# Block-sparse attention with a token and channel mixer: the first pair's copies on other engines, its gate in two banks, and a list made anew by a changed planner

## The chip, the cores and the metric

The kernel runs on one core of one Trainium2 chip. The metric is the device time of one execution in microseconds (us); lower is better. The kernel before took 246.04 us (median of three executions, 245.96 to 246.89).

The core has five instruction streams that run side by side and meet through semaphores: TensorE (PE in the profile; its weight loads are PEld), VectorE (DVE), ScalarE (ACT), GpSimd (POOL) and SyncE (SP), which here only starts transfers. Each stream is executed in the order in which it is written. GpSimd starts transfers too: those that turn 32-bit floats into 16-bit ones on the way.

## The reference

For each of 4 batches and 8 heads, q, k and v are 768 rows of 64 numbers. The 768 keys form 12 blocks of 64. A query may look at its own block and at the three earlier (or own) blocks whose mean key has the largest product with it. The heads' outputs, side by side, then go through a mixer over tokens and one over channels.

```python
k_rep = k.reshape(B, H, n_blocks, block, D).mean(axis=3)
gate_scores = np.einsum('bhsd,bhnd->bhsn', q, k_rep)
gate_scores = np.where(causal, gate_scores, -1000000000.0)
top_idx = np.argsort(gate_scores, axis=-1)[..., -top_k:]
...
scores = scale * np.matmul(q, k.transpose(0, 1, 3, 2))
mask = mask & (pos[:, None] >= pos[None, :])
scores = np.where(mask, scores, -1000000000.0)
...
return np.matmul(attn, v).astype(np.float32)
...
xt = x.transpose(0, 2, 1)
h = np.maximum(xt @ w_tok1, 0.0) @ w_tok2
u = x + h.transpose(0, 2, 1)
h2 = np.maximum(u @ w_ch1, 0.0) @ w_ch2
return (u + h2).astype(np.float32)
```

## The kernel before

Two heads of one batch form a pair, so there are 16 pairs; pairs 0 to 3 are batch 0. `pair(p)` describes the work of one pair, and `mlp(b)` the channel mixer of one batch, which needs the four pairs of that batch.

**A pair, step by step.** q and k come in as 32-bit tiles `q32` and `k32` (lines 508 and 516, by SP; for pair 0 half of them by ACT). v comes in through GpSimd's transfer as 16-bit `VA` (line 525). For the early pairs TensorE turns k and q over, in two halves of 384 columns each (`transposed`, line 446), into a PSUM tile `pm`. From there VectorE sums k's blocks of 64 (line 553, `ks`), and "spread" (line 534) writes the 12 sums of each head into a zeroed tile, so that one matmul serves both heads. `QT` (line 603) is q copied out of PSUM in 32 bits; `KA` and `QA` hold the 16-bit operands of the scores. `q16` (line 620) casts QT into QA. For pair 0 k goes from PSUM straight into KA (line 569); for later early pairs it goes through `k16` and is copied on to KA (line 573).

The gate is TensorE's product of QT and the block sums (line 639, into `g`), a bias add (line 643), VectorE's sorted eight largest (line 670), a comparison with the third largest (line 683, `bn`) and a memset that clears the own block (line 690). The result is turned over by TensorE (line 710) and copied into twelve further rows of QA (line 715), and KA's matching rows hold -30000 at their block, so the mask is part of the score matmul (line 731). ScalarE takes the exponential (line 744), GpSimd clears the upper triangle (line 752), TensorE multiplies with VA (line 761), and the token mixer follows (lines 779, 793, 807).

**Pair 0 is cut** (`CUT = 1`): each of these steps up to the gate runs in two halves of the sequence, so that the first can begin when half of k and q is there. Both halves of its gate lie in one PSUM bank `g`.

**The order is planned.** Nothing is issued as it is described. `P.op` records a step with the engines that may do it, a cost on each (time on the engine, time until its result is there, and for a transfer the time on the DMA engines), what it reads and writes, and a due time `pr`. `Plan.run` then simulates the engines and lists the steps: at each turn the engine that can start earliest takes its ready step with the smallest due time. The engines' instruction streams follow that list. Due times are a pair's own time `t0`, which advances by `EARLY` us for each of the first four pairs and by `PACE` after them, less a lead from the table `L` (`kd`, `qd`, `vd` for the loads of k, q, v; with an `e` in front for pairs 0 to 3). A step with `port=True` on VectorE shares one resource with GpSimd's steps in the simulation. In it all transfers, SP's and GpSimd's, follow each other in one line (`dma_free`). Where TensorE's list would leave a gap before the first channel mixer, `fill` puts matmuls of zeros (line 899), whose result nobody reads.

PSUM has two tiles of two banks for scores (`sc`) and four of one bank (`pm`) for everything else; a step that touches a `pm` or `sc` tile on one engine waits for the other engines' earlier steps on the same tile (`P.alone`).

Of the kernel before, what the change touches and what calls it, by code (L numbers as in the profile page):

```python
# [29 lines left out]
def _layout(groups):  # L30
    col, diag, width, base = {}, [], [], [0]
    for g, banks in enumerate(groups):
        mine, w = [], 0
        for bk, pieces in enumerate(banks):
# [17 lines left out]
EARLY, PACE = 5.78, 16.48  # L52
L = dict(kd=28.39, qd=24.29, vd=11.04, kt=13.4, kr=28.62, ke=-12.17, qt=24.03, qe=-10.99, q16=7.68, g=11.64, b=22.27,
         k16=20.14, r=24.99, w1=-9.34, w2=-3.8, wc1=11.98, wc2=30.18, tok=11.05, ml=12.98, o0=-2.69, o1=2.1, o2=2.23,
         o3=-0.75, o4=-2.45, o5=-0.39, o6=-3.33, o7=-8.31, o8=-1.83, o9=0.42, o10=-4.09, o11=-5.38, o12=6.03,
         o13=-1.8, o14=0.66, o15=3.06, m0=-0.25, m1=4.0, m2=6.99, m3=2.31, th=5.48, bd=5.16, cu=0.88, cs=5.86,
         ua=3.23, ub=23.41, ku=26.38, k0=5.54, k1=3.72, qu=23.81, dq=5.5, qp=5.5, dk=6.49, va=-11.68, ekd=26.02,
         eqd=24.07, evd=9.12, ekt=15.03, ekr=34.55, eke=-11.24, eqt=24.03, eqe=-6.62, eq16=4.03, eg=11.13, eb=22.27,
         etok=17.72)
# [28 lines left out]
class Plan:  # L88
# [6 lines left out]
    DMA = 1.1  # L95
    HELD = {"DVE": 115.0, "ACT": 130.0, "POOL": 85.0}
# [32 lines left out]
    def run(self, on_slot_end=None, fill=None):  # L129
        free = dict(FREE)  # L130
        dma_free, lanes = 0.0, [0.0] * self.LANES
# [30 lines left out]
        def start(o, e):  # L162
# [3 lines left out]
            if e in ("SP", "ACT") and len(o.cost[e]) > 2:  # L166
                t = max(t, lanes[0])
# [23 lines left out]
        while ready:  # L191
# [47 lines left out]
            if len(o.cost[e]) > 2:  # L239
                begin = max(dma_free, t + occ)  # L240
                dma_free = begin + o.cost[e][2] * self.DMA
                o.end = dma_free + lat
                if e != "POOL":
                    lanes.pop(0)
                    lanes.append(o.end)
# [54 lines left out]
def kernel(  # L300
# [11 lines left out]
    nc = tc.nc  # L312
# [110 lines left out]
    def weight(name, dst, src, n, each, pr, after):  # L423
        b = Buf(None)
        W[name] = (b, 0)
        P.op({"POOL": (800.0, 2200.0, n * each / 16.0)}, lambda: nc.gpsimd.dma_start(out=dst, in_=src), rd=[after], wr=[(b, 0)], pr=pr)

    def weights(after):
        weight("w1", w1, moe_w_tok1.rearrange("(j p) t -> p j t", p=128), 768, 60, L["w1"], after)
        weight("w2", w2, moe_w_tok2.rearrange("(g p) s -> p g s", p=128), 256, 135, L["w2"], after)  # L430
        for c in range(NCC):
            weight(("wc1", c), wc1[:, c, :], moe_w_ch1[128 * c:128 * c + 128, :], 128, 247, L["wc1"] + c, after)
        for f in range(0, NFC, 3):
            weight(("wc2", f), wc2[:, f:f + 3, :], moe_w_ch2[128 * f:128 * f + 384, :].rearrange("(g p) c -> p g c", p=128),
                   384, 98, L["wc2"] + f / 3, after)
# [46 lines left out]
    def pair(p):  # L482
# [38 lines left out]
        if p < 3:  # L521
# [3 lines left out]
        P.op({"POOL": (1100.0, 2200.0, 1536 * 16.0 / 16)}, lambda: nc.gpsimd.dma_start(  # L525
            out=VA.t[:, :, :, 0:64], in_=vs.rearrange("x (j p) d -> p x j d", p=128)), wr=[(VA, 0)], pr=t0 - lead["vd"], not_before=5000.0)

# [4 lines left out]
        def spread(e, z):  # L532
            for x in range(2):
                ENG[e].tensor_copy(out=ks2b.t[64 * x:64 * x + 64, x, z], in_=ks3.t[64 * x:64 * x + 64, 0, z])  # L534

        if straight_k:
# [6 lines left out]
            for x in range(2):  # L543
                P.op({"POOL": (772.0, 820.0), "ACT": (721.0, 825.0), "DVE": (470.0, 555.0)}, lambda e, x=x: copy(ENG[e], KA.t[0:64, x, :], KT.t[64 * x:64 * x + 64]),
                     port=True, rd=[(KT, 0), (KT, 1)], wr=[(KA, (x, 0)), (KA, (x, 1))], io=f"S{2 * x}>S0", pr=t0 - lead["ke"])
            if not thirds:
                P.op({"POOL": (380.0, 450.0), "DVE": (160.0, 240.0)}, lambda e: spread(e, slice(0, NB)), rd=[(ks3, 0), (ks3, 1)], wr=[(ks2b, 0), (ks2b, 1)], pr=t0 - lead["kr"] + 0.1, io="S0>S0 S2>S2")
# [395 lines left out]
```

## Time and profile before

| | |
|---|---|
| median of three executions | 246.04 us |
| the profiled execution's own time | 246.32 us |
| its span, first to last instruction | 244.6 us |
| TensorE / VectorE / ScalarE / GpSimd busy | 238.1 / 170.4 / 160.6 / 128.2 us |
| bytes read from and written to HBM | 29.01 / 8.45 MB |
| granted TensorE clock | 1.00 throughout |

The span leaves out 246.32 - 244.6 = 1.72 us of the execution that lie before its first instruction or after its last. In the profile's rows the first number is a start in us where the view is in order of time, "x3" is a count, a bracket at the end of a row is idle time of that engine just before the row and what ended it, and "L639" is line 639 of the kernel before. Copies that pass through one helper are recorded at its lines 342 (ScalarE) and 344 (VectorE, GpSimd).

### The profile page before, as it was taken

To read this page: it belongs to the slowest core of one execution; us is meant where nothing else is said; L and a number is where in the kernel's file an instruction comes from. 1 tells how busy PE (TensorE), PEld (TensorE's weight loads), DVE (VectorE), ACT (ScalarE), POOL (GpSimd) and SP (SyncE) were. 2 spreads that over 40 slices of the span, in tenths; PEclk is the share of its full clock that TensorE was granted. 3 is DMA by queue.
4 is the path that set the end of the run, shared out by engine and by line. 5 is a ranking of instruction groups with operands and counts; after the bars stand their busy time and mean duration, and the time that the engine had idled before them with its cause. 6 is when DMAs were issued, how large, how long until landed. Compare 5 with 4: busy or idle time off the path is not lost.

```text
span 244.6 us, 6642 instructions
## 1 busy us (share of the span) xinstructions
PE 238.1 (97%) x2467; PEld 162.9 (67%) x2467; DVE 170.4 (70%) x546; ACT 160.6 (66%) x251; POOL 128.2 (52%) x263
## 2 busy tenths in 40 slices
PE   7799999999999999999999999999999999999995
PEld 7588878897656676567575666567755766554644
DVE  3889887877879999999999889968385632202112
ACT  3786978759587696788988675589724672360620
POOL 6188778878487583978796747676102110000000
DMA  8999999999899897879999899510213211112103
GB/s 158 201 203 215 207 171 182 173 132 177 133 83 168 158 148 142 186 150 178 161 138 168 186 166 126 151 53 3 64 46 111 79 32 46 43 43 86 46 18 110
DMA packets 124120, 30.82 MB, mean 126 GB/s; under 512 B 117652, under 2 KB 120596, under 8 KB 124088
## 3 DMA queue, kind: packets, MB, share of 16 engines
q1 hardware_dynamic: 94400, 22.89, 46.7%
q0 software_dynamic: 28064, 7.08, 32.8%
q10 hardware_dynamic: 1624, 0.43, 0.9%
q8 instruction: 19, 0.31, 0.6%
q14 instruction: 13, 0.11, 0.2%
HBM read 29.01 MB, written 8.45 MB: 153 GB/s over the span
## 4 chain that ended last, share of the span: by engine, by line
PE 91%; DMA 3%; DVE 3%; issue 0%; SPq 0%; POOL 0%; POOLq 0%
PE pm L827 26%; PE pm L849 25%; PE sc L731 14%; PE pm L761 9%; PE pm L779 4%; PE pm L793 4%; DMA k<-in_k_dram 3%; PE pm L639 2%; PE pm L654 2%; PE pm L446 2%; PE pm L710 1%; PE pm L899 1%; DVE ks L553 1%; DVE ks L534 1%; PE pm L807 1%; DVE m L670 1%
## 5 line engine op out<-in xcount | busy, mean ns | idle before, releaser
L744 ACT ACTIVATE E<-sc 128x1024 f16<-128x1024 f32 (+2 forms) x96 | 84.0, 917 | 22.7 <-PE sc L731 21.3
L827 PE MATMUL pm<-uT,wc 128*128 128x384 f16 x384 | 69.9, 326 | 0.0
L849 PE MATMUL pm<-wc,h 128*128 128x512 f16 (+2 forms) x312 | 68.8, 363 | 0.0
L752 POOL TENSOR_SCALAR_AFFINE_SELECT E<-E 128x256 f16<-128x256 f16 (+1 forms) x96 | 39.2, 416 | 43.2 <-ACT E L744 41.4
L835 ACT ACTIVATE h<-pm 128x384 f16<-128x384 f32 x71 | 34.5, 491 | 28.2 <-PE pm L827 28.0
L827 PEld LDWEIGHTS <-wc 128*128 128x128 f16 x384 | 36.0, 98 | 22.5
L731 PE MATMUL sc<-QA,KA 76*128 76x512 f16 (+3 forms) x264 | 48.2, 301 | 0.3 <-DVE QA L344 0.3
L849 PEld LDWEIGHTS <-h 128*128 128x128 f16 x312 | 28.4, 98 | 26.0
L853 DVE TENSOR_TENSOR os<-u,pm 128x512 f32<-128x512 f16 (+2 forms) x26 | 16.6, 640 | 33.9 <-PE pm L849 33.2
L731 PEld LDWEIGHTS <-KA 76*128 76x128 f16 x264 | 23.6, 98 | 14.5 <-issue 0.4
L761 PEld LDWEIGHTS <-E 128*128 128x128 f16 x672 | 24.9, 98 | 3.6
L761 PE MATMUL pm<-VA,E 128*128 128x65 f16 x672 | 26.1, 193 | 0.0
L796 DVE TENSOR_TENSOR u<-x,pm 128x384 f16<-128x384 f16 x32 | 16.5, 542 | 4.7 <-PE pm L793 4.7
L837 DVE TENSOR_SCALAR h<-pm 128x384 f16<-128x384 f32 x25 | 13.8, 554 | 8.5 <-PE pm L827 7.5
L768 DVE TENSOR_TENSOR x<-pm,rc 128x384 f16<-128x384 f32 x32 | 17.8, 555 | 0.9
L525 POOL DMA_DIRECT2D VA<-in_v_dram x16 | 16.8, 1051 | 0.4 <-issue 0.3
L793 PE MATMUL pm<-h,w 128*128 128x128 f16 x192 | 13.8, 219 | 0.0
L342 ACT COPY QA<-bnt 12x384 f16<-12x384 f16 x20 | 10.2, 508 | 5.3 <-DVE bnt L695 4.9
L670 DVE MAX8 m<-gm 128x8 f32<-128x12 f32 x160 | 13.2, 156 | 0.5
L779 PE MATMUL pm<-x,w 128*128 128x128 f16 x192 | 13.3, 219 | 0.0
L793 PEld LDWEIGHTS <-w 128*128 128x128 f16 x192 | 11.9, 98 | 1.9
L779 PEld LDWEIGHTS <-w 128*128 128x128 f16 x192 | 11.7, 98 | 2.0 <-DVE x L768 0.4
(79 smaller groups left out, 302.2 us busy)
## 6 DMA issues: line engine op xcount, KB each, us to landing
out_dram<-os SPq DMA_DIRECT2D x22, 256.0 KB, 2.5
q<-in_q_dram SPq DMA_DIRECT2D x42, 96.0 KB, 2.9
k<-in_k_dram SPq DMA_DIRECT2D x38, 96.0 KB, 3.8
VA<-in_v_dram POOLq DMA_DIRECT2D x16, 192.0 KB, 6.0
wc<-in_moe_w_ch_dram POOLq DMA_DIRECT2D x8, 384.0 KB, 6.6
k<-in_k_dram SPq DMA_DIRECT2D x12, 192.0 KB, 5.6
turn<-k SPq DMA_DIRECT2D x11, 192.0 KB, 2.1
uT<-turn SPq DMA_DIRECT2D x44, 48.0 KB, 2.0
```

What stands on the lines that cost most here:

```text
L525: P.op({"POOL": (1100.0, 2200.0, 1536 * 16.0 / 16)}, lambda: nc.gpsimd.dma_start(out=VA.t[:, :, :, 0:64], in_=vs.rearrange("x (j p) d -> p ...
L731: nc.tensor.matmul(out=s.t[:, at:at + 128 * m], lhsT=KA.t[:, x, 128 * kk:128 * kk + 128], rhs=QA.t[:, q0:q0 + m, x, :], start=True, stop=True)
L744: nc.scalar.activation(out=E.t[:, BASE[g_]:BASE[g_ + 1]], in_=s.t[:, 0:WIDTH[g_]], func=AF.Exp, scale=scale)
L752: nc.gpsimd.affine_select(out=o, in_=o, pattern=[[0, len(d)], [1, 128]], compare_op=ALU.is_ge, fill=0.0, base=0, channel_multiplier=-1)
L761: nc.tensor.matmul(out=t[:, jq, :], lhsT=E.t[:, cc:cc + 128], rhs=VA.t[:, x, kk, :], start=(kk == 0), stop=(kk == jq))
L768: P.op(dve(384), lambda a=a, rc=rc, x=x: nc.vector.tensor_tensor(out=xp.t[:, :, 64 * x:64 * x + 64], in0=a.t[:, 0:NJ * 65].rearrange("p (j ...
L779: nc.tensor.matmul(out=m1.t[:, 128 * t:128 * t + 128], lhsT=w1[:, j, 128 * t:128 * t + 128], rhs=xp.t[:, j, :], start=(j == 0), stop=(j == ...
L793: nc.tensor.matmul(out=m.t[:, 128 * j:128 * j + 128], lhsT=w2[:, t, 128 * (j0 + j):128 * (j0 + j) + 128], rhs=h1.t[:, t, :], start=(t == 0 ...
L827: nc.tensor.matmul(out=m.t[:, 0:HS], lhsT=wc1[:, c, 128 * f:128 * f + 128], rhs=uT.t[:, c].rearrange("p (a w) -> p a w", a=4)[:, :, 96 * i ...
L835: nc.scalar.activation(out=o, in_=w, func=AF.Relu)
L849: nc.tensor.matmul(out=m.t[:, 0:wide], lhsT=h2.t[:, f, 128 * jj:128 * jj + 128], rhs=wc2[:, f, w:w + wide], start=(f == 0), stop=(f == NFC ...
L853: P.op(dve(wide), lambda j=j, m=m, o=o, w=w, wide=wide: nc.vector.tensor_tensor(out=o.t[:, w:w + wide].rearrange("p (c d) -> p c d", d=128 ...
```

## The change

Six edits, and then the list that the planner makes of them:

1. Pair 0's four casts of QT into QA (`q16`) are GpSimd's alone; before, VectorE or ScalarE took them.
2. Pair 0's copies of k out of PSUM into KA (`kev`) and of q into QT (`qev`) are ScalarE's alone; before, VectorE or ScalarE.
3. The two halves of pair 0's gate have a PSUM bank each (`gs`).
4. "Spread" on VectorE is a `tensor_reduce` over groups of one element, in place of a copy.
5. The step that loads v stands after q's copies in the description, and for pair 0 it waits for QT's second half; before, it waited for nothing but 5 us of simulated time.
6. The simulation has a line of its own for GpSimd's transfers (`cast_free`): such a transfer starts `PREPARE` = 1.2 us after its issue, and pushes back the transfers of SP that are still under way by its own length. Costs of several steps are set anew, `port` goes from two kinds of copy and their VectorE price from 470 to 870, `EARLY` goes from 5.78 to 4, many leads change, and the second half of pair 0's block sums has its own (`kr1`).

```diff
-EARLY, PACE = 5.78, 16.48
-L = dict(kd=28.39, qd=24.29, vd=11.04, kt=13.4, kr=28.62, ke=-12.17, qt=24.03, qe=-10.99, q16=7.68, g=11.64, b=22.27,
-         k16=20.14, r=24.99, w1=-9.34, w2=-3.8, wc1=11.98, wc2=30.18, tok=11.05, ml=12.98, o0=-2.69, o1=2.1, o2=2.23,
...
+EARLY, PACE = 4, 16.48
+L = dict(kd=28.39, qd=26.24, vd=9.53, kt=8.11, kr=35.36, ke=-11.57, qt=26.16, qe=-10.47, q16=13.67, g=12.55, b=18.91,
+         k16=22.64, r=24.99, w1=-9.34, w2=-6.45, wc1=11.98, wc2=27.86, tok=4.11, ml=12.0, o0=-2.91, o1=2.1, o2=2.23,
...
+    PREPARE = 1200.0
...
             if len(o.cost[e]) > 2:
-                begin = max(dma_free, t + occ)
-                dma_free = begin + o.cost[e][2] * self.DMA
-                o.end = dma_free + lat
-                if e != "POOL":
+                span = o.cost[e][2] * self.DMA
+                if e == "POOL":
+                    begin = max(cast_free, t + occ + self.PREPARE)
+                    cast_free = begin + span
+                    o.end = cast_free + lat
+                    for x in sent:
+                        if x.end - lat > begin:
+                            x.end += span
...
+                    dma_free = max(dma_free, begin) + span
+                else:
+                    dma_free = max(dma_free, t + occ) + span
+                    o.end = dma_free + lat
...
-        P.op({"POOL": (1100.0, 2200.0, 1536 * 16.0 / 16)}, lambda: nc.gpsimd.dma_start(
-            out=VA.t[:, :, :, 0:64], in_=vs.rearrange("x (j p) d -> p x j d", p=128)), wr=[(VA, 0)], pr=t0 - lead["vd"], not_before=5000.0)
...
             for x in range(2):
-                ENG[e].tensor_copy(out=ks2b.t[64 * x:64 * x + 64, x, z], in_=ks3.t[64 * x:64 * x + 64, 0, z])
+                if e == "DVE":
+                    nc.vector.tensor_reduce(out=ks2b.t[64 * x:64 * x + 64, x, z], in_=ks3.t[64 * x:64 * x + 64, 0, z].rearrange("c (n w) -> c n w", w=1), axis=AX.X, op=ALU.add)
+                else:
+                    nc.gpsimd.tensor_copy(out=ks2b.t[64 * x:64 * x + 64, x, z], in_=ks3.t[64 * x:64 * x + 64, 0, z])
...
-                    def kev(e, t=t, i=i, x=x):
-                        copy(ENG[e], KA.t[0:64, x, halves(i)], t.t[64 * x:64 * x + 64, 0:HS])
-                    P.op({**dve(HS), **act(HS)}, kev, rd=[(t, 0), (ks3, i)] if cut else [(t, 0)], wr=[(KA, (x, i))], io=f"P{2 * x}>S0", pr=at(i, lead["ke"]))
+                    def kev(t=t, i=i, x=x):
+                        nc.scalar.copy(out=KA.t[0:64, x, halves(i)], in_=t.t[64 * x:64 * x + 64, 0:HS])
+                    P.op(act(HS), kev, rd=[(t, 0), (ks3, i)] if cut else [(t, 0)], wr=[(KA, (x, i))], io=f"P{2 * x}>S0", pr=at(i, lead["ke"]))
...
-            P.op({**act(HS), **dve(HS)}, qev, rd=[(t, 0)], wr=[(QT, i)], io="P0>S0", pr=at(i, lead["qe"]))
+            P.op(act(HS) if cut else {**act(HS), **dve(HS)}, qev, rd=[(t, 0)], wr=[(QT, i)], io="P0>S0", pr=at(i, lead["qe"]))
...
+        P.op({"POOL": (1100.0, 650.0, 1536 * 14.0 / 16)}, lambda: nc.gpsimd.dma_start(
+            out=VA.t[:, :, :, 0:64], in_=vs.rearrange("x (j p) d -> p x j d", p=128)), rd=[] if p else [(QT, 1)], wr=[(VA, 0)], pr=t0 - lead["vd"], not_before=5000.0)
...
-                P.op({"DVE": (300.0, 380.0), "ACT": (410.0, 510.0)} if cut else {"POOL": (772.0, 820.0)} if p < L["qp"] else
-                     {"POOL": (772.0, 820.0), "ACT": (721.0, 825.0), "DVE": (470.0, 555.0)},
-                     q16, port=True, rd=[(QT, i)] if cut else [(QT, 0), (QT, 1)], wr=[(QA, (x, 0, i))], io=f"S{2 * x}>S0", pr=at(i, lead["q16"]))
+                P.op({"POOL": (430.0, 480.0)} if cut else {"POOL": (772.0, 820.0)} if p < L["qp"] else
+                     {"POOL": (772.0, 820.0), "ACT": (721.0, 825.0), "DVE": (870.0, 955.0)},
+                     q16, rd=[(QT, i)] if cut else [(QT, 0), (QT, 1)], wr=[(QA, (x, 0, i))], io=f"S{2 * x}>S0", pr=at(i, lead["q16"]))
...
-        g = Buf(Rr)
+        gs = [Buf(Rr) for _ in parts]
+        g = gs[0]
...
-                def gate(z0=z0, z1=z1, nb=nb):
+                def gate(z0=z0, z1=z1, nb=nb, g=gs[i]):
...
```

63 lines of the change are left out of this document (34 added, 29 removed).

## The prediction

> **What bounds the kernel now.** I read the page first, then the span cut into stages, the matmuls of zeros by stage, and the chain of waits in the first 20 us.
>
> ```profile
> PE 238.1 (97%) x2467; PEld 162.9 (67%) x2467; DVE 170.4 (70%) x546; ACT 160.6 (66%) x251; POOL 128.2 (52%) x263
> ```
>
> Busy time, share of the span and instructions by engine. TensorE is the bound, but 97% also counts the matmuls of zeros. The stages (length; busy us and instructions of PE, PEld, DVE, ACT and POOL; granted clock; DMA share; GB/s) show where it isn't:
>
> ```profile
> 5.00:14.00 9.00, 6.56 (x63) 5.28 (x62) 8.01 (x32) 6.86 (x14) 2.00 (x5) 1.00 1.45 205
> 20.00:30.00 10.00, 10.00 (x121) 8.75 (x117) 8.66 (x34) 7.71 (x11) 7.58 (x13) 1.00 1.34 211
> 56.00:240.00 184.00, 183.99 (x1750) 116.21 (x1748) 125.42 (x374) 120.25 (x189) 88.99 (x174) 1.00 0.66 109
> ```
>
> and so do the zeros of line 899 alone (PE and PEld busy, clock, DMA share, GB/s):
>
> ```profile
> 5.00:10.00 5.00, 0.91 (x11) 0.75 (x11) 1.00 1.54 197
> 10.00:15.00 5.00, 0.59 (x5) 0.40 (x5) 1.00 1.33 216
> 15.00:20.00 5.00, 0.60 (x5) 0.29 (x5) 1.00 1.32 201
> 20.00:25.00 5.00, 1.27 (x18) 1.08 (x18) 1.00 1.20 209
> 25.00:30.00 5.00, 1.43 (x21) 1.24 (x21) 1.00 1.47 212
> 40.00:60.00 20.00, 0.90 (x11) 0.67 (x11) 1.00 1.15 166
> ```
>
> From 56 us to 240 us TensorE idles 0.01 us, with no zeros: whatever the new list does to the other engines there, it can win nothing visible, and each us that the beginning saves is a us off the end. The beginning holds two stretches of slack. From 5 to 14 us it is 9.00 - 6.56 = 2.44 us idle and 0.91 + 0.59 = 1.50 us of zeros: **3.94 us**. From 15 to 30 us it is 0.60 + 1.27 + 1.43 = **3.30 us** of zeros, and 0.90 us more comes before the first channel mixer. Together 8.14 us: more than that the change cannot take out after the first 5 us, unless the useful work itself shrinks, and its matmuls stay the same in number.
>
> The chain of waits (start, us, what) says what the first stretch waits for:
>
> ```profile
> 4.15 5.64 DMA k<-in_k_dram
> 9.93 0.53 PE pm L446 x3
> 10.48 0.56 DVE ks L553
> 11.18 0.46 DVE k L344
> 11.64 0.47 DVE ks L553
> 12.14 0.53 DVE ks L534
> 12.69 0.90 DVE ks L534
> 13.58 0.27 DVE QA L344
> 13.89 0.98 PE sc L731 x7
> ```
>
> First pair 1's k, in flight for 5.64 us; then VectorE, one step after the other; and inside it two copies of twelve columns that take 0.53 and 0.90 us. Only from 13.89 us is TensorE fed.
>
> **Part 1: spread by a reduction.** What such small copies take elsewhere, what GpSimd did meanwhile, and two reductions:
>
> ```profile
> L534 DVE COPY ks<-ks 64x6 f32<-64x6 f32 x4 | 0.7, 165 | 0.1
> 11.79 0.82 POOL L344 COPY KA<-k 64x768 f16<-64x768 f16 x1 [0.19 <-DVE k L344]
> 12.56 0.51 POOL L752 TENSOR_SCALAR_AFFINE_SELECT E<-E 128x384 f16<-128x384 f16 x1
> L553 DVE TENSOR_REDUCE ks<-pm 128x6 f32<-128x384 f32 x14 | 7.3, 549 | 4.1 <-PE pm L446 4.1
> L541 DVE TENSOR_REDUCE ks<-KT 128x12 f32<-128x768 f32 x9 | 8.5, 942 | 0.3
> 12.18 0.52 PE L446 MATMUL pm<-id,q 128*128 128x128 f32 x3 [0.59 <-DMA q<-in_q_dram]
> ```
>
> A small copy takes 165 ns where nothing holds it; the slow two lie over a GpSimd copy (from 11.79 to 12.61 us) and a triangle step after it, and the first ends about when the GpSimd copy does. I read this as an access that the two engines share. A reduction's price follows from the last two rows: 384 more columns cost 942 - 549 = 393 ns, 1.02 ns each, so the fixed part is about 157 ns and twelve columns take some 170 ns. If a reduction doesn't need the shared access, two cost 0.34 us in place of 1.43: **1.09 us**; if it does, 0. I take 1.0 us of VectorE's chain, but only 0.6 us of TensorE's time, because the transposes of pair 1's q (12.18 us, last row) come 2.2 us after those of its k (9.93 us) and its gate needs both.
>
> **Part 2: casts, copies and banks of pair 0.**
>
> ```profile
> 6.37 0.51 ACT L342 CAST QA<-QT 64x384 f16<-64x384 f32 x1
> 6.38 0.55 DVE L344 CAST QA<-QT 64x384 f16<-64x384 f32 x1
> L344 POOL CAST QA<-QT 64x768 f16<-64x768 f32 x15 | 12.3, 819 | 0.9 <-ACT QT L342 0.5
> L342 ACT COPY QT<-pm 128x384 f32<-128x384 f32 x7 | 3.3, 486 | 0.3 <-PE pm L446 0.3
> L344 DVE COPY QT<-pm 128x384 f32<-128x384 f32 x5 | 2.7, 552 | 0.1
> 8.53 0.37 PE L639 MATMUL pm<-ks,QT 128*128 128x24 f32 x2 [0.71 <-DVE bn L683]
> 11.48 0.12 POOL L690 MEMSET bn<- 64x6 f16 x1
> ```
>
> VectorE loses two casts of 0.55 us and one QT copy of 0.552 us out of the 8.01 us that it is busy between 5 and 14 us: 1.65 us. ScalarE loses two casts (0.51 us each) and takes the copy at 0.486 us, so it does not grow. GpSimd gets four casts of half of 768 columns, between 0.41 us (half of 819 ns) and 0.82 us each; I take 0.43, 1.7 us in all, in the idle time before its row at 11.48 us (it is busy 2.00 of 9 us). If that cover were gone, the last cast would hold up the second half's scores by at most 0.8 us. The two banks remove the 0.71 us for which the second gate stood behind VectorE's comparison; 0 if QT's second half is late anyway, since it is copied at the same time. Of the 1.65 + 0.71 us I take 0.9 us on TensorE's path: the halves of pair 0's k and q land one after the other and set a floor under the rest.
>
> The Trainium skill speaks against handing casts to GpSimd: its page GPSIMD Engine Reference (section Key points) calls VectorE structurally about twice as fast for elementwise work. By that rule a cast would be 2 x 0.55 = 1.1 us, four of them 4.4 us, an estimate that would delay the second half's scores by some 2 us. The trace does not agree for this operation: 819 ns for twice the columns of VectorE's 0.55 us.
>
> **Part 3: v later, k and q earlier.**
>
> ```profile
> q1 hardware_dynamic: 94400, 22.89, 46.7%
> q0 software_dynamic: 28064, 7.08, 32.8%
> VA<-in_v_dram POOLq DMA_DIRECT2D x4, 192.0 KB, 7.4
> 3.31 1.19 POOL L525 DMA_DIRECT2D VA<-in_v_dram  x1
> 7.79 0.47 ACT L342 COPY QT<-pm 128x384 f32<-128x384 f32 x1
> 17.25 0.23 PE L761 MATMUL pm<-VA,E 128*128 128x65 f16 x2
> ```
>
> The first two rows (packets, MB, share of 16 engines over 244.6 us) make GpSimd's transfers dear: 32.8% x 244.6 / 7.08 MB = 11.3 us per MB, so one v of 192 KB takes 2.2 us of all the DMA engines. Before, pair 0's v is issued at 3.31 us, ahead of pair 1's k. Now it waits for QT's second half, which ends at 8.26 us, or some 7.5 us with part 2. Pair 1's k and q lose a neighbour worth between 0 (they arrive by their own queue's depth) and 2.2 us; I take 1.2, of which 0.8 us counts, since parts 1 and 2 partly free the same wait. Startup in all: 0.6 + 0.9 + 0.8 = **2.3 us of the 3.94**.
>
> The price: in the first 30 us a v lands 7.4 us after its issue (third row, median of four). Issued at 8 to 9 us it is there at 15.4 to 16.4 us. Its first user is at 17.25 us, and moves to 15.0 us if all else is 2.3 us earlier. TensorE would stand there for 0.4 to 1.4 us: I take **0.6 us** lost, because the list can put other matmuls ahead. GpSimd's casts and the own-block memset are what is queued behind that issue of 1.19 us on its stream; the second half's memset is due no sooner than 9 us, so nothing waits.
>
> **Part 4: the new order.** Leads and EARLY bring the loads of v for pairs 1 to 3 ahead of pair 5's k. The due times by the two tables: v of pair 1 from 5.78 + 2.1 - 9.12 = -1.2 to -3.0, of pair 2 from 4.7 to 1.1, of pair 3 from 7.5 to 3.5; k of pair 5 from 10.8 to 3.7, q of pair 3 ahead of k of pair 4 where it was behind. In the trace pair 1's v goes out late:
>
> ```profile
> 25.55 1.02 POOL L525 DMA_DIRECT2D VA<-in_v_dram  x1
> 34.67 1.49 PE L761 MATMUL pm<-VA,E 128*128 128x65 f16 x42
> ```
>
> so pair 1's product with v, due after the scores, runs at 34.67 us, and between 20 and 30 us TensorE multiplies zeros for 2.70 us. Moved up, 42 matmuls of the product would fill 1.4 us of them and its token mixer more. Against it stands that DMA is saturated there (1.34, 211 GB/s): what goes ahead pushes something else back. Bounds: all 3.30 us gained, or, if the waits move here from the startup, 2.3 us lost. I take **0.6 us** gained. The zeros before the first channel mixer stay; the later casts whose port and price change are 0.8 us each (row of 819 ns) beside a TensorE that never idles, so 0, and that is also what one would cost if it came due late.
>
> **Sum.** -2.3 + 0.6 - 0.6 = -2.3 us. Against the profiled execution: span 244.6 - 2.3 = 242.3, plus 1.72 around it, 244.0; that execution lies 0.28 us above the median, so for the median 246.04 - 2.3 = **243.7 us**.
>
> **The rivals.**
> *GpSimd's transfers don't go ahead* (slower). The simulation lets a v transfer start 1.2 us after issue and run alone: 1.1 + 1.2 + 1.34 x 1.1 + 0.65 = 4.4 us until it is there, where the row above has 7.4. TensorE takes its list in order, so a product listed 4.4 us behind its load stands for up to 3.0. It decides once the list places a product less than 7.4 us after its v's issue with nothing in between. For pairs 0 and 1 that costs 3.0 us each and for pair 2, when the rush is ending, half as much: 7.5 us. Of these 2.7 take the place of zeros that stand there now, and 2.3 are what the start gains; 2.5 us remain: 248.5 us. Against it: the product at 17.25 us has no idle time before it now. The Trainium skill's page DMA: Bandwidth & Descriptors, section Issuing engines are not separate DMA queues, says that transfers from all engines share the same 16 DMA engines and interleave: by that, no transfer of GpSimd truly goes ahead, which is this rival's mechanism. The trace agrees: a DMA share of 1.34 between 20 and 30 us means packets of more than one transfer at a time on each engine.
> *DMA decides.* k, q and v of four pairs are the same bytes at 205 to 211 GB/s; TensorE is fed sooner but runs dry sooner, and the zeros of 15 to 30 us grow by most of what the start saves: 245.5 us. For it: a DMA share over 1 in each window quoted above up to 60 us. Against it: pairs 4 and 5 are loaded early now, and can move back.
> *Both stretches close.* The start gains 2.9 and the second stretch 2.0 us: 241.1 us.
> *The edits change nothing on the path*, since pair 1's landing alone sets 9.79 us: 246.0.
>
> **Chances.** Forecast 0.46 (242.6 to 244.8), DMA decides 0.20, both close 0.12, GpSimd's transfers 0.18, nothing 0.04. Half a percent, about what a measurement of this kernel can tell from no change, is 1.2 us, so faster is below 244.8: 0.45 of the forecast, 0.12, and 0.02 of the second rival, 0.59. Same gets the rest of it, the fourth and a little of the slower one: 0.24. Slower keeps 0.17. The range goes from the case where both close to a milder form of the slower one, with 1.6 us lost in place of 2.5: 241.0 to 247.6 us, with the forecast's own 242.6 to 244.8 inside.
>
> **What would show it.** Part 1: the spread rows of pair 1 at 0.2 us beside a busy GpSimd. Part 2: no idle time before the second gate; GpSimd casts of about 0.43 us. Part 3: pair 1's k landing before 9 us, the first score matmuls two us earlier, and little idle time before the first product with v. Part 4: fewer zeros from 15 to 30 us. I am wrong if TensorE idles before line 761 for over 2 us, if zeros from 15 to 56 us grow past 6 us, or if idle time appears after 56 us.

## The result, and the profile after

| | before | after |
|---|---|---|
| median (executions) | 246.80 us (6) | **253.12 us** (6) |
| lowest and highest | 245.96, 251.62 | 251.88, 254.25 |
| profiled execution, span | 246.32, 244.6 | 251.88, 250.2 |

The ratio is 1.0265 [1.0224, 1.0306]: slower, and above the predicted range of 241.0 to 247.6 us. Here and below the ratios leave out executions that lie over 1.5% above the fastest of their kernel (before, the one of 251.62 us), and the medians keep them. In the kernel after, the lines that the prediction names lie further down: scores L748, exponential L761, product with v L778, load of v L627, second token matmul L810, zeros L916, copies L355 (ScalarE) and L357 (VectorE, GpSimd).

The page of the kernel after, engines:

```profile
PE 237.4 (95%) x2432; PEld 160.9 (64%) x2432; DVE 174.0 (70%) x541; ACT 159.2 (64%) x249; POOL 128.2 (51%) x270
```

TensorE is busy 0.7 us less in a span that is 5.6 us longer. Matmuls of zeros fell from 9.12 to 6.73 us (both rows over the whole span):

```profile
0.00:250.00 250.00, 9.12 (x103) 7.60 (x103) 1.00 0.79 123
```
```profile
0.00:250.00 250.00, 6.73 (x68) 5.58 (x68) 1.00 0.79 123
```

So of the 5.6 us, idle time is +6.25 (12.75 in place of 6.5) and busy time -0.65. The zeros' 2.4 us can't be taken off the busy time one for one: the rows of single lines overlap, and add up to 286.6 us before, where TensorE is busy for 238.1. The stages of the kernel after (columns as in the prediction) show where it idles:

```profile
5.00:14.00 9.00, 8.31 (x83) 7.02 (x82) 6.30 (x30) 6.81 (x13) 5.27 (x12) 1.00 1.30 220
14.00:40.00 26.00, 20.90 (x278) 17.01 (x277) 20.08 (x80) 17.54 (x25) 19.04 (x31) 1.00 1.64 188
56.00:200.00 144.00, 141.02 (x1482) 92.05 (x1479) 123.08 (x367) 102.83 (x156) 87.97 (x180) 1.00 0.82 129
```

The first row is the gain that was forecast, in part: 0.69 us idle, where it was 2.44, so 1.75 of 2.3 us (the zeros there stay, 1.70 us where they were 1.50). The other two are the loss: 26.00 - 20.90 = **5.10 us** idle from 14 to 40 us and 144.00 - 141.02 = **2.98 us** from 56 to 200 us. The same two stretches before:

```profile
14.00:40.00 26.00, 25.84 (x339) 21.83 (x337) 21.81 (x93) 20.52 (x29) 21.57 (x39) 1.00 1.57 193
56.00:200.00 144.00, 143.99 (x1504) 94.11 (x1502) 118.18 (x362) 106.41 (x161) 88.99 (x174) 1.00 0.81 126
```

0.16 and 0.01 us. Zeros from 14 to 40 us fell from 3.30 to 1.67 us, so some of the idle time only takes their place: idle time and zeros together went from 3.46 to 6.77 us. What TensorE waits for after the change (in total, times, longest), and some of its rows before 40 us:

```profile
PE pm L778 <- DMA VA<-in_v_dram: 3.8, 3, 1.7
PE pm L778 <- DVE u L813: 2.0, 1, 2.0
PE pm L810 <- DMA w<-in_moe_w_tok_dram: 1.2, 1, 1.2
```
```profile
7.83 0.85 PE L656 MATMUL pm<-ks,QT 128*128 128x24 f32 x6 [0.20 <-ACT QT L355]
...
8.84 0.87 PE L459 MATMUL pm<-id,k 128*128 128x128 f32 x6
...
9.55 0.83 PE L748 MATMUL sc<-QA,KA 76*128 76x256 f16 x10
...
22.43 1.51 PE L778 MATMUL pm<-VA,E 128*128 128x65 f16 x42 [1.16 <-DMA VA<-in_v_dram]
...
30.42 0.51 PE L810 MATMUL pm<-h,w 128*128 128x128 f16 x6 [1.20 <-DMA w<-in_moe_w_tok_dram]
...
33.91 1.49 PE L778 MATMUL pm<-VA,E 128*128 128x65 f16 x42 [1.71 <-DMA VA<-in_v_dram]
...
36.77 0.83 PE L778 MATMUL pm<-VA,E 128*128 128x65 f16 x21 [0.94 <-DMA VA<-in_v_dram]
```

The start is 1.1 us earlier (pair 1's k is turned at 8.84 us, 9.93 before), but the first product with v goes from 17.25 to 22.43 us, and still waits. GpSimd's stream says why:

```profile
14.47 0.82 POOL L357 CAST QA<-QT 64x768 f16<-64x768 f32 x1
15.24 0.83 POOL L357 COPY KA<-k 64x768 f16<-64x768 f16 x1
16.01 1.19 POOL L627 DMA_DIRECT2D VA<-in_v_dram  x1
...
19.69 0.84 POOL L439 DMA_DIRECT2D w<-in_moe_w_tok_dram  x1
...
25.89 1.03 POOL L627 DMA_DIRECT2D VA<-in_v_dram  x1
```

Pair 0's v is issued at 16.01 us, behind pair 1's casts. Pair 1's v, which the change was to bring forward, goes out no earlier than before (25.55 us then), the first token weight later (14.81), and the second, for which TensorE waits, at 22.11 us (21.64). The 2.0 us in the second stretch are here, VectorE and GpSimd side by side:

```profile
128.01 0.42 POOL L769 TENSOR_SCALAR_AFFINE_SELECT E<-E 128x256 f16<-128x256 f16 x1
...
128.23 3.41 DVE L357 CAST QA<-QT 64x768 f16<-64x768 f32 x1
...
128.39 1.26 POOL L625 TENSOR_TENSOR R<-QT 128x640 f32<-128x640 f32 x1
...
129.98 1.24 POOL L664 TENSOR_TENSOR R<-R 128x640 bf16<-128x640 f32 x1
...
131.17 1.10 POOL L627 DMA_DIRECT2D VA<-in_v_dram  x1
131.57 1.00 DVE L813 TENSOR_TENSOR u<-x,pm 128x384 f16<-128x384 f16 x2
...
132.16 0.82 PE L778 MATMUL pm<-VA,E 128*128 128x65 f16 x21 [2.00 <-DVE u L813]
```

A cast that takes 0.56 us elsewhere lasts until GpSimd's chain of steps ends, and the sums behind it on VectorE (`u`) come so late that TensorE stands 2.00 us.

### The profile page after: what moved, and what is told of

Read it like the earlier page. It is cut to its first block, busy times and chain, and to the rows that moved or that the text cites. A ratio compares the mean times of both kernels' runs of the same rounds, so it can differ in the third digit from the quotient of the medians.

```text
span 250.2 us, 6570 instructions
## 1 busy us (share of the span) xinstructions
PE 237.4 (95%) x2432; PEld 160.9 (64%) x2432; DVE 174.0 (70%) x541; ACT 159.2 (64%) x249; POOL 128.2 (51%) x270
## 4 chain that ended last, share of the span: by engine, by line
PE 75%; DMA 10%; DVE 5%; issue 3%; ACT 2%; POOL 1%; SPq 1%; ACTq 0%; DVEq 0%
PE pm L844 24%; PE pm L866 22%; PE sc L748 11%; PE pm L778 7%; DMA VA<-in_v_dram 6%; PE pm L796 4%; PE pm L810 3%; DMA q<-in_q_dram 2%; ACT E L761 2%; DMA k<-in_k_dram 2%; PE pm L459 1%; PE pm L671 1%; DVE h L854 1%; DMA uT<-turn 1%; DVE m L687 1%
## 5 line engine op out<-in xcount | busy, mean ns | idle before, releaser
L761 ACT ACTIVATE E<-sc 128x1024 f16<-128x1024 f32 (+2 forms) x96 | 84.1, 917 | 24.3 <-PE sc L748 23.0
L852 ACT ACTIVATE h<-pm 128x384 f16<-128x384 f32 x74 | 36.1, 490 | 29.7 <-PE pm L844 29.3
L748 PE MATMUL sc<-QA,KA 76*128 76x512 f16 (+3 forms) x264 | 48.5, 301 | 0.4 <-ACT E L761 0.4
L748 PEld LDWEIGHTS <-KA 76*128 76x128 f16 x264 | 23.6, 98 | 14.2 <-issue 0.6
L778 PE MATMUL pm<-VA,E 128*128 128x65 f16 x672 | 26.1, 193 | 6.1 <-DMA VA<-in_v_dram 3.8
L778 PEld LDWEIGHTS <-E 128*128 128x128 f16 x672 | 24.9, 98 | 10.0 <-issue 5.8
L627 POOL DMA_DIRECT2D VA<-in_v_dram x16 | 16.9, 1054 | 0.1
L781 DVE RECIPROCAL rc<-pm 128x6 f32<-128x6 f32 x32 | 6.0, 187 | 14.3 <-PE pm L778 14.2
L357 POOL CAST QA<-QT 64x768 f16<-64x768 f32 (+1 forms) x17 | 13.3, 780 | 4.3 <-ACT QT L355 3.8
L854 DVE TENSOR_SCALAR h<-pm 128x384 f16<-128x384 f32 x22 | 12.1, 551 | 4.6 <-PE pm L844 2.3
L810 PE MATMUL pm<-h,w 128*128 128x128 f16 x192 | 13.8, 219 | 1.2 <-DMA w<-in_moe_w_tok_dram 1.2
L810 PEld LDWEIGHTS <-w 128*128 128x128 f16 x192 | 12.1, 98 | 3.4 <-DMA w<-in_moe_w_tok_dram 1.4
## 6 DMA issues: line engine op xcount, KB each, us to landing
out_dram<-os SPq DMA_DIRECT2D x22, 256.0 KB, 2.1
```

Source lines behind the costliest of these rows:

```text
L627: P.op({"POOL": (1100.0, 650.0, 1536 * 14.0 / 16)}, lambda: nc.gpsimd.dma_start(out=VA.t[:, :, :, 0:64], in_=vs.rearrange("x (j p) d -> p ...
L748: nc.tensor.matmul(out=s.t[:, at:at + 128 * m], lhsT=KA.t[:, x, 128 * kk:128 * kk + 128], rhs=QA.t[:, q0:q0 + m, x, :], start=True, stop=True)
L761: nc.scalar.activation(out=E.t[:, BASE[g_]:BASE[g_ + 1]], in_=s.t[:, 0:WIDTH[g_]], func=AF.Exp, scale=scale)
L778: nc.tensor.matmul(out=t[:, jq, :], lhsT=E.t[:, cc:cc + 128], rhs=VA.t[:, x, kk, :], start=(kk == 0), stop=(kk == jq))
L810: nc.tensor.matmul(out=m.t[:, 128 * j:128 * j + 128], lhsT=w2[:, t, 128 * (j0 + j):128 * (j0 + j) + 128], rhs=h1.t[:, t, :], start=(t == 0 ...
L852: nc.scalar.activation(out=o, in_=w, func=AF.Relu)
```

## The experiments

All ratios are against the kernel before, run on the same chip (medians 246.6 to 248.0 us). Differences between kernels are taken from ratios, 1% being 2.5 us. Idle time is TensorE's in the profiled execution, from windows as above.

| run | kernel | us | ratio |
|---|---|---|---|
| e4 | before + pair 0's engines, banks, reduction | 244.5 | 0.9895 [0.9842, 0.9948] |
| e5 | before + reduction alone | 245.9 | 0.994 [0.9917, 0.9963] |
| e11 | e4 + new prices and ports | 246.0 | 0.9966 [0.9936, 0.9995] |
| e10 | e4 + new line for GpSimd's transfers | 248.2 | 1.003 [0.9996, 1.0064] |
| e12 | e4 + new table | 255.1 | 1.0215 [1.0135, 1.0295] |
| e17 | e4 + table, first four pairs' half | 252.5 | 1.0145 [1.0072, 1.0217] |
| e18 | e4 + table, later pairs' half | 249.2 | 1.0092 [1.0061, 1.0122] |
| e7 | after, old line | 250.5 | 1.0148 [1.0079, 1.0218] |
| e8 | after, old table | 249.4 | 1.0089 [1.0052, 1.0127] |
| e1 | after, v of pair 0 first on GpSimd | 254.8 | 1.0285 [1.0211, 1.036] |
| e13 | after, v of pair 0 due before q of pair 2 | 256.0 | 1.0348 [1.0304, 1.0392] |
| e14 | e12, the same due time | 257.2 | 1.0197 [1.0108, 1.0287] |
| e16 | e13, and token weights due as early | 254.6 | 1.0219 [1.0147, 1.0291] |
| e15 | e13, transfers planned to land after 8.0 us | 253.7 | 1.0213 [1.0148, 1.0279] |
| e2 | after, GpSimd's first six transfers moved up | 249.5 | 1.0091 [1.0054, 1.0128] |
| e3 | after, five late casts by ScalarE | 250.6 | 1.0138 [1.0097, 1.0178] |
| e6 | e2 and e3 | 247.1 | 1.0023 [0.9984, 1.0063] |
| e9 | after, zeros ahead of four waiting steps | 253.2 | 1.023 [1.0185, 1.0275] |

### The edits without the new list

e5 takes the reduction alone; e4 adds the engines of pair 0's casts and copies and its two gate banks, with the old simulated line, prices and leads.

```diff
-ENG[e].tensor_copy(out=ks2b..., in_=ks3...)
+nc.vector.tensor_reduce(out=ks2b..., in_=ks3...)        # e5 and e4, on VectorE
-P.op({**dve(HS), **act(HS)}, kev, ...)
+P.op(act(HS), kev, ...)                                  # e4; qev alike
-{"DVE": (300.0, 380.0), "ACT": (410.0, 510.0)} if cut
+{"POOL": (430.0, 480.0)} if cut                          # e4
+gs = [Buf(Rr) for _ in parts]                            # e4
```

> The kernel before with one edit: VectorE's spread is a reduction in place of a copy (same list). If the copies wait for an access that GpSimd holds and a reduction doesn't need it: pair 1's two rows at 0.2 us in place of 0.53 and 0.90, and 245.4 to 246.0 us beside 246.0 to 246.5 of the kernel before. If a reduction waits as well or they are slow for themselves: rows of 0.5 us or more, no difference.

> The kernel before, with its planner, costs and due times, and of the change only the engines of pair 0's casts and copies, the gate's two banks and the spread by reduction. If these edits are good and the list alone costs the time: 244.0 to 245.8 us, TensorE fed by 12 to 13 us, no new waits for v. If the edits themselves cost it (GpSimd slower at casts, ScalarE overloaded, its transfers of v behind them): 247.5 us or more.

Both are faster than before, as expected. e4's stages:

```profile
5.00:14.00 9.00, 8.59 (x82) 7.49 (x81) 6.08 (x30) 7.26 (x15) 6.30 (x12) 1.00 1.49 207
14.00:40.00 26.00, 25.55 (x339) 21.44 (x339) 21.22 (x93) 21.03 (x30) 21.66 (x41) 1.00 1.64 196
56.00:200.00 144.00, 143.99 (x1512) 94.18 (x1511) 117.59 (x361) 105.95 (x160) 87.58 (x172) 1.00 0.78 124
```

The start is as full as after the change, and neither of the two later stretches idles. **e4 beats both kernels**: what makes the kernel after slow is in the planner's part.

### The planner's three parts, one at a time

e11 gives e4 the new prices and takes `port` from two kinds of copy; e10 gives it the new line for GpSimd's transfers; e12 the new table. In all three v's load also stands where the change puts it (edit 5).

```diff
-                     {"POOL": (772.0, 820.0), "ACT": (721.0, 825.0), "DVE": (470.0, 555.0)},
-                     q16, port=True, ...
+                     {"POOL": (772.0, 820.0), "ACT": (721.0, 825.0), "DVE": (870.0, 955.0)},
+                     q16, ...
```
```diff
-                begin = max(dma_free, t + occ)
-                dma_free = begin + o.cost[e][2] * self.DMA
+                    begin = max(cast_free, t + occ + self.PREPARE)
+                    cast_free = begin + span
...
-        P.op({"POOL": (1100.0, 2200.0, 1536 * 16.0 / 16)}, ...
+        P.op({"POOL": (1100.0, 650.0, 1536 * 14.0 / 16)}, ...
```
```diff
-EARLY, PACE = 5.78, 16.48
-L = dict(kd=28.39, qd=24.29, vd=11.04, kt=13.4, kr=28.62, ke=-12.17, qt=24.03, qe=-10.99, q16=7.68, g=11.64, b=22.27,
+EARLY, PACE = 4, 16.48
+L = dict(kd=28.39, qd=26.24, vd=9.53, kt=8.11, kr=35.36, ke=-11.57, qt=26.16, qe=-10.47, q16=13.67, g=12.55, b=18.91,
...
```

> The good kernel (244.5 us) and of the planner's changes only the prices: port gone from two kinds of copy, 870 for them on VectorE, and the small price changes. If the missing port is what holds up VectorE: casts of QT into QA on VectorE of 1.3 us or more beside GpSimd's steps, at least one of them ahead of a wait of TensorE, 245.5 to 248 us. If the cast of 3.41 us was bad luck of that one list: 244 to 245 us, no wait over 0.5 us after 56 us.

> The good kernel (before, with pair 0's edits and the spread, 244.5 us) and of the planner's changes only the simulated line for GpSimd's transfers; prices, port, due times as before. If the simulation alone makes the list too hopeful: TensorE waits 1 to 2 us for v between 20 and 40 us, 246 to 248 us. If it is harmless alone: 244 to 245 us.

> The good kernel (244.5 us) and of the planner's changes only the due times: L, EARLY, kr1. If they put pair 0's v behind GpSimd's copies for pair 1: v issued at about 16 us, its first product waits, and 246 to 249 us. If they are good and only the other two parts spoil the list: 243 to 245 us.

Over e4, the prices cost 0.7% (little more than the intervals allow), the line 1.35% and the table **3.2%**, more than either case expected. In e10 TensorE did not wait for v but 1.2 us for a token weight and 2.4 us, at 116 us, for a step of VectorE. e7 and e8 undo the line (second diff) and the table (third diff) from the other side, in the kernel after.

> The changed kernel with the old simulation of transfers (one line for all, GpSimd's results 2.2 us later, old lengths) and the new table, EARLY, costs and edits of pair 0. If the simulated transfers make the list too hopeful: no wait of TensorE for v or a token weight over 0.5 us, and 247 to 250 us (the late cast may remain). If the new due times are to blame: the waits for v stay, 252 us or more.

> The changed kernel with the due times and EARLY of the kernel before; the new simulation, costs and edits of pair 0 stay. If the simulated transfers make the list too hopeful: TensorE still waits over 2 us for v and token weights, 250 us or more. If the new due times are to blame: no such waits, 247 us or less.

The undone line saves 1.2% and the undone table 1.8%. Both came out between their two cases: one wait for v stayed in each, of 2.1 and 1.9 us. The parts don't add up: 5.25% one by one, 3.7% together. But the medians fall into two groups: 244.5 to 249.4 us with the old table, 250.5 to 257.2 us with the whole new one and nothing moved by hand. What of the prices is felt can be seen in VectorE's casts of QT (shortest, median, longest ns), in e11, where `port` is gone, and in e12, where it stays:

```profile
L345 DVE CAST QA<-QT x6: 531/736/2850, 57.2 to 161.3; 64x768 f16<-64x768 f32 x6
```
```profile
L345 DVE CAST QA<-QT x5: 542/556/816, 61.5 to 171.6; 64x768 f16<-64x768 f32 x5
```

With `port` kept (e4, e10, e12, e14, e17, e18) none took over 1.3 us; without it the longest took 0.87 us in e8, 2.85 in e11 and 3.41 in after. A held cast costs TensorE only where a step that it needs soon stands behind: in e11 all idle time from 56 to 200 us is 0.36 us.

e17 and e18 split the table: EARLY, the leads with an `e`, o0 to o3, cu, kr1, w2 and wc2 in e17; the others in e18.

```diff
-EARLY, PACE = 5.78, 16.48
+EARLY, PACE = 4, 16.48
-L = dict(... eqd=24.07, ekr=34.55, eke=-11.24, eqe=-6.62, eq16=4.03, eg=11.13, etok=17.72 ...)
+L = dict(... eqd=25.89, ekr=37.94, eke=-13.29, eqe=-7.22, eq16=2.64, eg=13.71, etok=19.71 ...)
```

> Pair 0's edits with the old simulated line and old prices, and of the new table only what concerns the first four pairs: EARLY = 4, their leads, their offsets, the lead of the second half's sums and the due times of the weights. If the loss arises where the first pairs' loads are placed, 250 to 255 us, with TensorE idle for over 2 us between 14 and 40 us and little idle time after 56 us. If it arises in the later pairs' leads, 244.5 to 247 us.

> The other half of the table: the later pairs' leads and offsets, with EARLY = 5.78 and the first four pairs as before. If the loss is the beginning's, 244.5 to 247 us; if it is made after 56 us, 248 us or more, with TensorE idle for over 2 us after 56 us.

e17, then e18:

```profile
14.00:40.00 26.00, 22.98 (x286) 19.32 (x285) 17.45 (x75) 18.18 (x28) 21.01 (x36) 0.93 1.52 193
56.00:150.00 94.00, 91.84 (x957) 60.31 (x954) 79.27 (x236) 72.67 (x110) 67.39 (x128) 0.98 1.03 152
```
```profile
14.00:40.00 26.00, 25.44 (x332) 21.16 (x331) 20.68 (x92) 20.26 (x30) 21.99 (x42) 1.00 1.54 196
56.00:150.00 94.00, 91.44 (x965) 59.96 (x964) 80.40 (x246) 72.38 (x109) 67.38 (x129) 1.00 1.12 164
```

The first pairs' half empties the beginning (3.02 us idle, and a granted clock of 0.93). The later pairs' half leaves it full (0.56 us), and yet TensorE idles 2.56 us after 56 us, where it never idled. Each half has a loss of its own: 2.5% over e4 in e17, 2.0% in e18. That e17 idles after 56 us too (2.16 us), against the expectation, would fit EARLY, from which the later pairs' due times count on; no run separates that.

Part of the loss comes with a lower clock. e17's six executions took 249.3 and 249.5 us at a mean clock of 1.0, and 252.2 to 254.1 us at 0.98 to 0.986; e12's four took 250.7 us at 1.0 and 254.3 to 256.1 us at 0.973 to 0.978. So some 5 to 6 us over e4 are lost at full clock too (in e12 by one execution), and 3 to 5 us more come where it falls.

### Which place in the order

e1 keeps the list of after and moves one load in it; the others change due times and have everything listed anew.

```diff
+    for name, by in [(("v", 0), 99000.0)]:
+        o = casts[name]
+        order.remove(o)
+        order.insert(next(i for i, x in enumerate(order) if x.eng == "POOL" and x not in casts.values() and x.start >= o.start - by), o)
```
e13, e15, e16 (in after) and e14 (in e12):
```diff
-pr=t0 - lead["vd"], not_before=5000.0)
+pr=t0 - lead["vd"] - (3.7 if p == 0 else 0.0), not_before=5000.0)
```
e16, and then e15, besides:
```diff
-768, 53, L["w1"], after)
+768, 53, -13.4, after)
-256, 119, L["w2"], after)
+256, 119, -13.2, after)
```
```diff
-        P.op({"POOL": (1100.0, 650.0, 1536 * 14.0 / 16)}, ...
+        P.op({"POOL": (1100.0, 4250.0, 1536 * 14.0 / 16)}, ...
```

> The changed kernel's list, step for step, but the issue of pair 0's v stands first on GpSimd's stream, as in the kernel before. Late transfers (the list issues GpSimd's transfers too late for the products that need them): the wait of 1.2 us at pair 0's product with v goes, and the time falls by about 1.3 us from 253 us. DMA decides (its engines are full, so an earlier v only makes k and q later): pair 1's k lands 1 to 2 us later, the first score matmuls come later than 9.6 us, and the time stays within 0.5 us of 253.

> The planner lets transfers start in the order of their due times. By the new table the loads of q of pair 2 (due -15.66), k of pair 4 (-13.87) and k and q of pair 3 (-13.44, -13.31) are due ahead of pair 0's v (-12.03); by the old one v (-11.81) stood ahead of all of them (-10.28, -7.72, -9.43, -7.48). Here v alone gets a due time between pair 2's k and q (-15.73), and everything is listed anew. If that place is the step that failed, v is issued at 8.3 to 8.6 us, the wait of 1.16 us before the first product goes, and the time is 250 to 251 us. If the new order as a whole is at fault (weights, v of pairs 1 to 3), v is issued as early, but the waits at 30 to 37 us stay and the time is 252 to 253 us.

> The kernel with the new table alone (old simulated line, old prices; 255.1 us) with the same due time for pair 0's v. If v's place is what makes the table dear, 249 to 251 us and v issued at 8.3 to 8.6 us. If other entries of the table are, 253 us or more with v issued as early.

> The kernel after with the due times of pair 0's v and of the two token weights set so that they stand among the loads of k and q where they stood before the change (-15.73, -13.4, -13.2). If the order of transfers is the cause, the wait of 1.2 us for a token weight goes too, and the time is 1 to 2 us below that of the kernel with v's due time alone, 248 to 249.5 us. If it isn't, the two agree within 0.7 us.

> The kernel after with that due time, and GpSimd's transfers planned to be there 8.0 us after their issue (the measured median of the first 40 us) in place of 4.4. If products listed too early behind their loads are a cause of their own, the waits for v at 30 to 37 us go (0.94 to 1.71 us each) and the time is 1.5 to 3 us below that of the kernel with the due time alone. If the list has nothing else to put ahead of them, zeros or other waits take their place, and the two times agree within 0.7 us.

My theory of v's place missed. In e1 the load goes out ahead of pair 1's k, and TensorE waits 0.84 us for that k:

```profile
10.18 1.51 PE L459 MATMUL pm<-id,k 128*128 128x128 f32 x6 [0.84 <-DMA k<-in_k_dram]
```

e14 is no better than e12 (1.0197 and 1.0215). In e13 v is out at 8.54 us and the first product runs at 15.65 us without a wait, yet the kernel is 0.8% *slower* than after:

```profile
15.65 0.83 PE L778 MATMUL pm<-VA,E 128*128 128x65 f16 x21
...
27.31 0.84 PE L796 MATMUL pm<-x,w 128*128 128x128 f16 x12 [1.67 <-DVE QA L357]
...
30.91 0.88 PE L810 MATMUL pm<-h,w 128*128 128x128 f16 x12 [0.80 <-DMA w<-in_moe_w_tok_dram]
...
34.73 2.47 PE L778 MATMUL pm<-VA,E 128*128 128x65 f16 x42 [2.75 <-DMA VA<-in_v_dram]
```

What the start gains is waited away later: pair 1's v, issued at 24.35 us, lets its product run at 34.73 us, where it ran before too (34.67). e15 and e16 gain 1.35 and 1.3% on e13, for e15 a little more than was expected, for e16 clearly more, but not for its reason: the wait for a token weight stayed (1.3 us). Against after neither is a difference (the intervals overlap). In e16's profiled execution the beginning is fuller, and the loss elsewhere:

```profile
14.00:40.00 26.00, 24.52 (x325) 20.76 (x324) 21.16 (x92) 18.39 (x26) 21.91 (x42) 1.00 1.51 195
56.00:200.00 144.00, 137.50 (x1422) 89.81 (x1421) 111.39 (x348) 98.88 (x149) 85.05 (x166) 0.99 0.84 122
```

6.50 us are idle after 56 us. That execution took 256.88 us, and the three that e16's ratio counts 251.77 to 253.64 us; how much of the idle time they share is not shown. An early place for pair 0's v does not by itself win the time back; and since e13 to e16 list everything anew, they don't price that place alone.

### The waits themselves, removed from the list of after

e2 keeps that list and moves only GpSimd's first six transfers up in its stream (pair 0's v to its front, the others by 5 to 6 us of the plan, with the lines of e1); e3 keeps it and gives VectorE's five casts of QT to ScalarE; e6 does both, with pair 0's v behind pair 0's casts.

```diff
+    for name, by in [(("v", 0), 99000.0), ("w1", 6000.0), ("w2", 5000.0), (("v", 1), 6000.0), (("v", 2), 6000.0), (("v", 3), 6000.0)]:
...
+    for o in turnable:
+        if o.eng == "DVE":
+            o.eng = "ACT"
```

> The changed kernel's list, but the issues of GpSimd's first six transfers (v of pairs 0 to 3, the two token weights) stand earlier on its stream: pair 0's v first, the others some 5 planned us sooner. Late transfers: the four waits of TensorE for v and a token weight (1.16, 1.20, 1.71 and 0.94 us, 5.0 in all) shrink to under 1.5 us and the time falls by 3 to 4.5 us, to about 249.5. DMA decides: the waits move to k and q, idle time between 20 and 40 us stays near 5 us, and the time falls by less than 1 us.

> The changed kernel's list, but the five casts of QT into QA that it gives to VectorE from pair 6 on are done by ScalarE at the same places. Held access (VectorE's cast of 3.41 us at 128 us waits for GpSimd's steps, because the planner no longer keeps the two apart): that cast becomes 0.83 us on ScalarE, TensorE's wait of 2.0 us at 132 us goes, and the time falls by 1.8 to 2.3 us from 253. Rival (that wait is for v, as the wait before a product with v can be): the 2.0 us stay and the time is within 0.5 us.

> The changed kernel's list with GpSimd's six first transfers issued earlier (pair 0's v behind pair 0's casts, so that pair 1's k goes ahead of it) and the five late VectorE casts given to ScalarE. If the two causes are separate, their gains add: 3.5 + 2.3 us from 253, so about 247, and with pair 1's k undisturbed 246. If they are one (the early waits shift the later work), about 249.

They gain 1.7, 1.3 and, together, 2.4% on after, e2 and e6 what was expected, e3 a little more. From 14 to 40 us e2 has the first loss closed, and the second still open; e3 has the second nearly closed; windows of e2, then e3:

```profile
14.00:40.00 26.00, 26.00 (x341) 22.15 (x340) 20.81 (x95) 21.84 (x32) 22.10 (x38) 0.98 1.41 189
56.00:200.00 144.00, 141.91 (x1474) 92.42 (x1472) 121.58 (x354) 103.89 (x157) 86.11 (x175) 1.00 0.80 128
```
```profile
100.00:150.00 50.00, 49.86 (x524) 32.01 (x522) 43.34 (x124) 41.31 (x62) 36.77 (x73) 1.00 1.25 165
```

So either loss can be closed while the other stays, and their places are shown: GpSimd's transfers too far back in its stream (14 to 40 us), VectorE's casts beside GpSimd's steps (128 us). The transfers have to move together; v of pair 0 alone (e1) does not do it.

Two things remain. Where GpSimd's transfers go out earlier, TensorE waits longer for k (0.3 us after the change), as the rival *DMA decides* has it, only for less than is gained. In e2, then e6 (in total, times, longest):

```profile
PE pm L459 <- DMA k<-in_k_dram: 1.4, 2, 1.2
```
```profile
PE pm L459 <- DMA k<-in_k_dram: 2.0, 1, 2.0
```

And with both losses treated e6 is back at the time before, but 1.3% behind e4. Where these 3.2 us go is open.

### Zeros in the waits

e9 adds 24 matmuls of zeros, whose result nobody reads, at each of four places: ahead of the first product of pairs 0 to 2 and of the second token matmul of pair 0.

```diff
+for _ in range(24):
+    nc.tensor.matmul(out=a.t[:, 392:512], lhsT=zero, rhs=zero[:, 0:120], start=True, stop=True)
```

> The changed kernel, list untouched, with 24 matmuls of zeros on TensorE ahead of the first product with v of pairs 0, 1 and 2 and of pair 0's second token matmul, where it now stands idle. They write 120 unused columns of the product's own bank and need neither v nor the weight. If idle time lowers the granted clock afterwards (a wait costs twice): no window with a clock under 0.9, every execution's mean clock at 0.99 or above, and 250.5 to 252 us. If the clock falls for another reason: it falls as often as before (mean 0.98 to 0.99 in most executions) and the time is 253 us or more, since the zeros take up to 1.3 us each where no wait is left.

TensorE is busy 9.65 of the 10 us from 30 to 40 us (6.93 after), the clock of six executions is 0.993 to 1.0 (0.98 to 0.999 after), and the time is the same, 253.2 us (intervals overlap). In the two profiled executions, both at a clock of 0.999, the first product of pairs 0 and 1 runs at 22.76 and 34.03 us (22.43 and 33.91 after): the arrival of data sets this stretch. What a lower clock alone costs this run can't say, since the zeros take time of their own where no wait is left.

## Why the prediction was wrong

**Part 1 was right in its mechanism, and its gain too small.** The reduction over 12 elements takes 157 ns (170 forecast); in e5 pair 1's two take 0.33 us beside GpSimd's copy, where the copies took 1.43. Alone it gains 0.6% in e5, 1.5 us where 0.6 was forecast. In the kernel after, the new list gave this very step to GpSimd:

```profile
11.56 0.42 POOL L547 COPY ks<-ks 64x12 f32<-64x12 f32 x2
```

**Part 2 was right.** GpSimd's half casts take 501 ns, nearer to the lower bound of 0.41 than to 0.82, and the wait before the second gate went from 0.71 to 0.20 us. For half a cast GpSimd is as quick as VectorE (0.55 us); for a whole one it is not (819 ns, and VectorE's best 542 ns, in e12). Parts 1 and 2 under the old planner (e4, where v goes out at 8.53 us too) gain 1.05%, 2.6 us, where the start was to gain 2.3.

**Part 3: right in its direction, wrong in its price, and beside the point.** Pair 1's k is turned 1.1 us earlier, and the first scores come at 9.55 us in place of 10.61 (two us were forecast). "Issued at 8 to 9 us it is there at 15.4 to 16.4 us" holds where it is issued then: in e4 it stands behind pair 0's casts, goes out at 8.53 us, and the product runs at 15.58 us. In the kernel after it is issued at 16.01: I worked out the new due times of pairs 1 to 3's v, and not that the table moves four loads of k and q ahead of pair 0's v (-12.03 against -15.66 to -13.31, in the expectation above). But in e13 mending this due time gains nothing.

**Part 4 is the step that failed.** "Moved up, 42 matmuls of the product would fill 1.4 us of them": the due times moved, the issue of pair 1's v did not (25.55 to 25.89 us). So in place of 0.6 us gained, idle time and zeros from 14 to 40 us grew by 3.3 us, and 5.1 us are idle. Of the rivals this was the slower one, with the right mechanism (a product listed too close behind its load) and 248.5 us: TensorE is ready for the products of pairs 0 and 1 at 5.3 and 6.3 us after the issue of their v, and the median from issue to landing is 8.0 us before 40 us, near the 7.4 of the row that the rival used:

```profile
VA<-in_v_dram POOLq DMA_DIRECT2D x5, 192.0 KB, 8.0
```

What that rival had too small is the chance (0.18) and a second loss. "Beside a TensorE that never idles, so 0" was a price from the wrong side: a stretch without idle time can gain nothing from a new list, but it can lose. I wrote the first half of that sentence and gave the second no term. It cost 2.98 us, 2.0 of them behind one cast of 3.41 us; casts that long were found only where `port` no longer keeps them apart from GpSimd's steps in the simulation. Moving the five casts to ScalarE (e3) takes the 2.0 us away.

Two of the three signs for being wrong came ("TensorE idles before line 761 for over 2 us", "idle time appears after 56 us"): 3.8 and 2.98 us. The third did not: zeros from 15 to 56 us fell from 4.21 to 1.67 us, and so did those from 15 to 30 us that Part 4 wanted fewer, but idle time grew instead.

Open is which single lead costs what, and what holds e6 1.3% above e4. The runs show that both halves of the table cost (2.5 and 2.0% over e4), not which entry.

## What to carry to other kernels

Judge local edits and a re-made order apart: here the edits gain 1% and the new order loses 3.7%. Where the bounding engine has no idle time, a new order has no gain to win and any late step to lose, so it needs a term of loss and a rival of its own. A transfer's due time is not its issue: read what stands ahead of it on the issuing engine's stream and, where transfers go in order of due time, recompute every due time that the change passes it by.

## What the hardware showed beside that

**The granted clock can fall after short gaps.** In e1, TensorE by single us (busy, granted clock, DMA share, GB/s):

```profile
8.00:9.00 1.00, 0.74 (x6) 1.00 1.42 223
9.00:10.00 1.00, 0.34 (x3) 0.95 1.43 232
10.00:11.00 1.00, 0.82 (x4) 0.50 1.26 211
...
15.00:16.00 1.00, 1.00 (x10) 0.50 1.13 235
16.00:17.00 1.00, 1.00 (x9) 0.64 1.11 216
17.00:18.00 1.00, 1.00 (x12) 1.00 0.60 133
```

About 1.1 us of idle time within three were followed by some 6.8 us at half the clock. The Trainium skill (TensorE: Matmul & The Clock Gate, HAM oscillation — how this bites in real kernels) warns of idle gaps of more than about 3.4 us; here only shorter ones stand ahead of the fall. They don't always bring it: in the profiled execution of after TensorE idles 2.90 of the 5 us from 29 to 34 us at a clock of 1.00, and one list differs between executions (after: 0.999 once, 0.98 to 0.986 five times). The clock doesn't explain by itself how far executions of one list lie apart: those of e9, with the clock up, go from 251.2 to 253.6 us.

**One VectorE cast can be held by several GpSimd steps in a row.** Five casts of QT by VectorE took 556 ns at best and 3409 ns at worst:

```profile
L357 DVE CAST QA<-QT x5: 556/1367/3409, 64.0 to 141.7; 64x768 f16<-64x768 f32 x5
```

The Trainium skill (SBUF — State Buffer, Who interferes with whom) has, where both engines use the ports that they share, the later one blocked for the other's whole instruction; at 128.23 us the cast outlasted the step then running and three more, until GpSimd issued a transfer. The runs show these times; that a shared port is the reason they don't show.
